# Two interleaved transformer layers on one core: a planner that keeps ACT and DVE apart in a PSUM bank, last weights placed behind the last strips, and one boot V pass moved to steps 5 to 7

## The chip, the cores and the metric

The kernel runs on one core of one Trainium2 chip. The metric is the device time of one launch in microseconds (us). A core has five engines that run their own instruction queues in order and wait for each other through semaphores: PE (TensorE, with weight loads listed apart as PEld), DVE (VectorE), ACT (ScalarE), POOL (GpSimd) and SP (SyncE). In this kernel SP and POOL issue the DMA transfers. PE writes only to PSUM, which is cut into eight banks here; ACT and DVE read the banks.

## The reference

Two layers of the same kind are applied one after the other to x, 2048 rows of 512 bfloat16 numbers. Each layer is a recurrent attention with memory (A) and a gated feed-forward block (B), both behind a layernorm:

```
for s in range(n_seg):                       # 64 segments of 32 rows, in order
    h = concat([mem, x[s]])                  # 8 memory rows + 32 rows = 40 rows
    q, k, v = h@Wq, h@Wk, h@Wv               # 32 heads of 128
    p = softmax(mask(q k^T * scale))
    o = (p @ v) @ Wo
    mem = o[:8]; out[s] = o[8:]
x = x + A(layernorm(x)); x = x + B(layernorm(x))   # B: (sigmoid(h Wg) * (h Wu)) Wd, F = 1792
x = x + A(layernorm(x)); x = x + B(layernorm(x))
```

The memory makes the 64 segments a chain: segment s+1 cannot start before the first eight rows of segment s are out.

## The kernel before, in words

**Steps.** A step t computes segment t of the first layer and, 6 steps later in time, segment t-6 of the second layer in the same matmuls (`emit_step`). So there are 70 steps. Steps 0 to 5 and 64 to 69 carry one layer (40 columns in each matmul), steps 6 to 63 carry both (80 columns). In a step, the 32 heads go in six groups (five of 6 heads, one of 2). For each group: q and k (L721), a copy of their bank by ACT, scores (L735), mask and softmax on DVE and ACT (L748 to L780), transposition of p (L794) and a copy, p times v (L807) and a copy, and the product with Wo (L824), which all groups gather in one bank, WB. At the end of a step DVE copies the memory rows from WB to the next step's hT (L837 for two layers, L842 for one), and ACT copies the other rows from the same bank to oxT (recorded as L1017, since every plain copy is issued there on ACT and at L1019 on DVE).

**v.** The rows of v that depend on the memory are made in the step itself by the "strips" (`add_strips`, L693, 32 matmuls): two banks, two copies to sst, and four DMAs on SP (L702) that lay the rows into the v tiles vsb. The rows that depend on x alone are made ahead by V passes (`v_pass`, L583): 128 rows of v at a time in eight chunks of 512 columns, four matmuls each, then a copy and a DMA to a scratch tensor scr in HBM, from which SP loads them to vsb when their step comes (L681). Nine V passes of the first layer (twelve of its sixteen blocks, in three groups of four, `v_group`) are "boot" passes: they use the nine weight tiles of the feed-forward block as staging (pool bootp, two chunks to a tile) and their DMAs go on SP or POOL. The first loads of feed-forward weights wait for these tiles. The other V passes use the small tiles vst (three of them, one chunk each) and SP.

**Feed-forward.** After every fourth step of a layer a block of 128 rows goes through `ffn`: transposes (L891), layernorm (`layernorm_T`: DVE L539 to L543, a power on POOL at L542, PE transposes L552), gate and up (L923), activation, down (L947). Weights come by DMA from POOL (L915, L916, L941) in a ring of three tiles of each kind. For the first layer, a layernorm and a V pass for the second layer follow. The last block of the second layer is done in two parts (the first three quarters while step 69 runs, the last quarter after it), with its weights all loaded once (`last_weights`, L871): nine into the ring tiles and twelve into the tile wv_sb of Wv, which is free once step 69's strips have read it.

**What sets the order.** All of this is written as tasks with engine, duration and dependencies, and a list scheduler (`Planner`) lays out the order of every engine's instructions: `forward` gives a free engine the ready task with the longest tail, with PSUM banks and buffers handed out as they come free; `backward` refines the tails; 24 rounds, and the order with the shortest plan is taken. A task's keys r and w are only the planner's view of it. The semaphore waits in the program come from the tiles that an instruction really touches and from the order. Where two engines read one bank, the program makes the second wait for the first, which this planner does not know; it only counts an extra 240 ns (`late=240.0`, L849) for the ACT copy of WB. Feed-forward and V-pass tasks without a near deadline are what fills PE while a step waits for its softmax.

Of the kernel before, what the change touches and what calls it, by code (L numbers as in the profile page):

```python
# [10 lines left out]
F32 = mybir.dt.float32  # L11
# [5 lines left out]
P = 128  # L17
MEM = 8
SEG = 32
# [7 lines left out]
BLK = 4  # L27
# [22 lines left out]


class Task:
    __slots__ = ("eng", "dur", "lat", "fn", "deps", "succ", "tail", "boost", "ndep", "ready", "start", "idx", "on", "fresh", "acq", "rel", "durs", "tick", "prev", "land", "adj")

    def __init__(self, eng, dur, lat, fn, boost):
        self.durs = dur if isinstance(dur, dict) else {e: dur for e in eng}
        self.eng, self.dur, self.lat, self.fn, self.boost = eng, min(self.durs.values()), lat, fn, boost
        self.deps, self.succ, self.fresh = set(), [], set()
        self.acq, self.rel = [], []
        self.on = None  # L60
        self.land = 3000.0
        self.adj = {}


class Buf:

    __slots__ = ("pool", "kind", "users", "first", "left", "slot", "t_free", "t_prev")

    def __init__(self, pool, kind):
        self.pool, self.kind = pool, kind  # L70
# [4 lines left out]


class Pool:
    def __init__(self, tiles, caps=None):
        self.tiles, self.caps = tiles, caps or {}
        self.free = [(0.0, None, i) for i in range(len(tiles))]  # L80
        self.used = {}


class Planner:
# [18 lines left out]
    def add(self, eng, dur, fn, r=(), w=(), lat=None, boost=0.0, use=(), late=0.0):  # L103
        engs = eng if isinstance(eng, tuple) else (eng,)
        tk = Task(engs, dur, self.LAT[engs[0]] if lat is None else lat, fn, boost)
        tk.idx = len(self.tasks)
        for k in r:
            if k in self.writer:
                tk.deps.add(self.writer[k])
                tk.fresh.add(self.writer[k])  # L110
        for k in w:
            if k in self.writer:
                tk.deps.add(self.writer[k])
            for q in self.readers.get(k, ()):
                tk.deps.add(q)
        for k in w:
            self.writer[k] = tk.idx
            self.readers[k] = []
        for k in r:
            self.readers.setdefault(k, []).append(tk.idx)  # L120
        tk.deps.discard(tk.idx)
        if late:
            tk.adj = {d: late for d in tk.fresh if self.tasks[d].eng == ("PE",)}
        self.tasks.append(tk)
        for k in list(r) + list(w) + list(use):
            if isinstance(k, Buf) and (not k.users or k.users[-1] != tk.idx):
                k.users.append(tk.idx)
        return tk
# [78 lines left out]
    def forward(self):  # L207
        T = self.tasks
        for bf in self.bufs:
            bf.first, bf.left, bf.slot, bf.t_free = None, len(set(bf.users)), None, 0.0  # L210
            bf.pool.free = [(0.0, None, i) for i in range(len(bf.pool.tiles))]
            bf.pool.used = {}
            bf.pool.last = {}
# [36 lines left out]
        while left:  # L250
            while events and events[0][0] <= now:
                _, kind, i = heapq.heappop(events)
                if kind == 0:
                    for e in T[i].eng:
                        heapq.heappush(ready[e], (-T[i].tail, i))
            did = False
            for e in free:
                if free[e] > now:
                    continue
                h, aside, tk = ready[e], [], None  # L260
                while h:
                    q = heapq.heappop(h)
                    if T[q[1]].on is not None:
                        continue
                    if T[q[1]].acq and not fits(T[q[1]], now):
                        aside.append(q)
                        continue
                    tk = T[q[1]]
                    break
                for q in aside:  # L270
                    heapq.heappush(h, q)
                if tk is None:
                    continue
                did = True
                tk.on, tk.start, tk.dur = e, now, tk.durs[e]
                seq[e] += 1
                tk.tick = seq[e]
                for bf in tk.acq:
                    pool = bf.pool
                    q = min((q for q in pool.free if self.slot_at(q, tk) <= now), key=lambda q: q[0])  # L280
                    pool.free.remove(q)
                    bf.slot = q[2]
                    tk.prev += pool.last.get(q[2], [])
                    pool.last[q[2]] = sorted(set(bf.users))
                    pool.used[bf.kind] = pool.used.get(bf.kind, 0) + 1
                end = now + tk.dur
                if self.waits(tk, seen[e]) > 1 and e in ("DVE", "ACT"):
                    end += self.WAIT
                free[e] = end
                if e == "SP":  # L290
                    lanes.append(end + tk.land)
                    if len(lanes) >= 8:
                        free[e] = max(end, lanes[-8])
                heapq.heappush(events, (free[e], 1, 0))
                for bf in tk.rel:
                    bf.left -= 1
                    if end >= bf.t_free:
                        bf.t_free, bf.first = end, tk
                    if bf.left == 0:
                        bf.pool.free.append((bf.t_free, bf.first, bf.slot))  # L300
                        bf.pool.used[bf.kind] -= 1
                        heapq.heappush(events, (bf.t_free + bf.first.lat + self.TO_PE, 1, 0))
                        heapq.heappush(events, (bf.t_free + bf.first.lat, 1, 0))
                order.append(tk)
                left -= 1
                for s in tk.succ:
                    n = T[s]
                    n.ready = max(n.ready, end + self.gap(tk, n))
                    n.ndep -= 1
                    if n.ndep == 0:  # L310
                        release(n)
            if not did and left:
                while events and events[0][0] <= now:
                    _, kind, i = heapq.heappop(events)
                    if kind == 0:
                        for e in T[i].eng:
                            heapq.heappush(ready[e], (-T[i].tail, i))
                        did = True
                if did:
                    continue  # L320
                assert events, "no task can go on"
                now = events[0][0]
# [24 lines left out]
class Kern:  # L347
# [49 lines left out]
    def setup_tiles(self):  # L397
# [43 lines left out]
        self.wd = [c.tile([P, 2, D], BF16, name=f"wd{i}") for i in range(self.ND)]  # L441
        self.lns = [c.tile([P, 12], F32, name=f"lns{i}") for i in range(3)]
        pp = ctx.enter_context(tc.tile_pool(name="ps", bufs=1, space=PSUM))
        self.bank = Pool([pp.tile([P, 512], F32, name=f"bank{i}") for i in range(8)], {"bg": 3, "v": 3})
        self.qkp = Pool(self.qku)
        self.vstp = Pool(self.vst)
        self.sstp = Pool(self.sst)
# [154 lines left out]
    def v_group(self, blocks, psts, boot=False):  # L602
# [5 lines left out]
        for b, cut in zip(blocks, cuts):  # L608
            pst, B = psts[b] if b in psts else self.ln_x(b)
            for q, c0, r0, n in cut:  # L610
                xi = (base + q) % 2
                pcs[q].append((c0, 0, b, r0, n))
                self.take_v(pst, B, 0, self.xvf[xi], [("xvf", xi, g) for g in range(c0 // 32, (c0 + 4 * n) // 32)], c0, r0, n)
            for q in range(3):
                if sum(4 * x[4] for x in pcs[q]) == P:
                    xi = (base + q) % 2
                    self.v_pass(self.xvf[xi], [("xvf", xi, g) for g in range(4)], pcs[q], boot)
                    pcs[q] = []

    def load_x(self, b, xb, key, boost=None):  # L620
# [28 lines left out]
    def emit_step(self, t):  # L649
# [194 lines left out]
        for idx, j in enumerate(jobs):  # L844
# [1 line left out]
            b = s // BLK  # L846
            oi = b % 2
            dst = self.oxT[j][oi][:, :, (s % BLK) * SEG:(s % BLK + 1) * SEG]
            pl.add("ACT", 160, lambda dst=dst, a=48 * j - c0: (dst, wo3(a, SEG)), r=[WB], w=[("oxT", j, oi, s % BLK)], late=240.0)  # L849

    def last_weights(self):

        if self.lw is None:
# [3 lines left out]
            for jp in range(self.FC // 2):  # L857
                row = []
                for nm, ring, n in (("wg", self.wg, self.NG), ("wu", self.wu, self.NG), ("wd", self.wd, self.ND)):
# [8 lines left out]
                        keys = keys + [own]  # L868
                        k += 1
                    src = self.wdv[:, 2 * jp:2 * jp + 2, :] if nm == "wd" else (self.wgv if nm == "wg" else self.wuv)[:, :, jp * 2 * P:(jp + 1) * 2 * P]  # L870
                    pl.add("POOL", 760, lambda tl=tl, src=src: nc.gpsimd.dma_start(out=tl[:, :, :], in_=src), w=keys, lat=6000.0)  # L871
                    row.append((tl, own))
                self.lw.append(row)
        return self.lw
# [94 lines left out]

    def trace(self):  # L970
        self.fill = {}
        self.lw = None
        self.clear()
        p0 = self.pre1(0)
# [12 lines left out]
        for t in range(self.NSTEPS):  # L987
            if t % BLK == 0 and t and t // BLK + 1 < self.NBLK:
                self.pre1(t // BLK + 1)
            self.emit_step(t)  # L990
            if t % BLK == BLK - 1 and t < self.NSEG:
                b = t // BLK
                if b % 3 == 0 and b <= 9:
# [83 lines left out]
```

## Time and profile before

| | |
|---|---|
| Median of 4 runs | 1859.58 us (1858.24 to 1860.54) |
| The profiled execution | 1860.49 us, its span 1858.7 us, mean granted PE clock 0.997 |
| PE busy | 1817.9 us, 98% |
| PEld, DVE, ACT, POOL busy | 1576.1, 1274.7, 1174.0, 570.6 us |
| Step start to step start, two layers, steps 18 to 21 | 23.2, 23.3, 26.6, 31.1 us |
| Step start to step start, one layer, steps 1 to 3 and 66 to 68 | 20.8, 20.1, 22.5 and 19.6, 18.9, 18.5 us |
| Step 69's strips to the end of the span | 39.6 us |

A step's start is the start of its first strips matmul (L693). "Busy" adds the records of an engine; PE's matmuls overlap in their pipeline, so a busy PE can still run below its best rate. How much it runs below is seen from the start-to-start time of matmuls of one kind: 72 q and k matmuls of 80 columns take 2.58 us in the chain of the profile, which is 35.8 ns each.

### The profile page before, as it was taken

To read this page: it belongs to the slowest core of one execution; us is meant where nothing else is said; L and a number is where in the kernel's file an instruction comes from. 1 tells how busy PE (TensorE), PEld (TensorE's weight loads), DVE (VectorE), ACT (ScalarE), POOL (GpSimd) and SP (SyncE) were. 2 spreads that over 40 slices of the span, in tenths; PEclk is the share of its full clock that TensorE was granted. 3 is DMA by queue.
4 is the path that set the end of the run, shared out by engine and by line. 5 is a ranking of instruction groups with operands and counts; after the bars stand their busy time and mean duration, and the time that the engine had idled before them with its cause. 6 is when DMAs were issued, how large, how long until landed. Compare 5 with 4: busy or idle time off the path is not lost.

```text
span 1858.7 us, 94041 instructions
## 1 busy us (share of the span) xinstructions
PE 1817.9 (98%) x41066; PEld 1576.1 (85%) x41282; DVE 1274.7 (69%) x4115; ACT 1174.0 (63%) x2748; POOL 570.6 (31%) x821
## 2 busy tenths in 40 slices
PE   8999999999999999999999999999999999999998
PEld 3678788888888898989888898989888888989786
DVE  5456566776677667767677777767677667767564
ACT  6665666666666666666666656666666666665553
POOL 4214023222424142323424142323424132324223
PEclk9999999999999999999999999999999999999998
DMA  9625234454645454554645364554645454545434
GB/s 350 231 77 166 77 98 135 138 155 129 177 129 167 120 166 125 151 150 131 182 129 166 104 182 120 150 153 127 184 127 163 120 163 120 155 141 159 143 101 132
DMA packets 128438, 273.79 MB, mean 147 GB/s; under 512 B 26882, under 2 KB 59402, under 8 KB 128026
## 3 DMA queue, kind: packets, MB, share of 16 engines
q0 software_dynamic: 56848, 183.48, 33.5%
q1 hardware_dynamic: 71178, 84.29, 15.9%
q8 instruction: 323, 5.29, 1.2%
q14 instruction: 89, 0.73, 0.1%
HBM read 221.85 MB, written 27.26 MB: 134 GB/s over the span
## 4 chain that ended last, share of the span: by engine, by line
PE 90%; SPq 3%; DVE 2%; DMA 2%; ACT 2%; issue 1%; POOL 0%; ACTq 0%; POOLq 0%; DVEq 0%
PE bank L721 32%; PE bank L824 16%; PE bank L923 11%; PE bank L693 7%; PE bank L583 7%; PE bank L735 5%; PE bank L794 4%; PE bank L947 4%; PE bank L807 4%; SPq L491 2%; PE bank L552 1%; DMA wk_sb<-in_A_Wk_dram 1%; DMA vsb<-sst 0%; DMA wv_sb<-in_A_Wv_dram 0%; PE bank L891 0%
## 5 line engine op out<-in xcount | busy, mean ns | idle before, releaser
L721 PE MATMUL bank<-hT,wq_sb 128*128 128x80 bf16 (+1 forms) x8960 | 622.1, 198 | 2.3 <-ACT hT L1017 0.7
L721 PE MATMUL bank<-hT,wk_sb 128*128 128x80 bf16 (+1 forms) x8960 | 621.1, 198 | 1.3 <-issue 1.1
L1017 ACT CAST qku<-bank 128x480 bf16<-128x480 f32 (+3 forms) x770 | 394.5, 512 | 251.7 <-PE bank L721 224.5
L721 PEld LDWEIGHTS <-wq_sb 128*128 128x128 bf16 x8960 | 458.6, 99 | 27.1 <-DVE hT L837 3.5
L721 PEld LDWEIGHTS <-wk_sb 128*128 128x128 bf16 x8960 | 450.6, 99 | 1.7 <-issue 1.2
L748 DVE TENSOR_TENSOR st<-bank,maskb 80x240 f32<-80x240 f32 (+1 forms) x732 | 269.7, 369 | 224.4 <-PE bank L735 212.5
L824 PE MATMUL bank<-otsb,wo_sb 128*128 128x80 bf16 (+1 forms) x8960 | 367.4, 198 | 6.8 <-ACT otsb L1017 3.8
L824 PEld LDWEIGHTS <-wo_sb 128*128 128x128 bf16 x8960 | 338.5, 99 | 23.7 <-issue 6.9
L915 POOL DMA_DIRECT2D wg<-in_B_w_gate_dram x217 | 165.0, 760 | 492.2 <-PE bank L923 439.2
L1017 ACT CAST otsb<-bank 128x480 bf16<-128x480 f32 (+3 forms) x420 | 200.6, 487 | 91.1 <-PE bank L807 72.1
L777 DVE TENSOR_TENSOR pb<-st,rz 80x480 bf16<-80x480 f32 x348 | 206.3, 593 | 5.5 <-PE bank L794 0.3
L760 DVE TENSOR_REDUCE sm<-st 80x6 f32<-80x240 f32 (+3 forms) x420 | 153.3, 365 | 75.3 <-ACT st L758 73.2
L542 POOL TENSOR_TENSOR lns<-lns,negh 128x1 f32<-128x1 f32 (+1 forms) x79 | 44.2, 561 | 519.6 <-DVE lns L541 432.5
L941 POOL DMA_DIRECT2D wd<-in_B_w_down_dram x217 | 153.7, 710 | 158.0 <-PE bank L735 66.2
L1017 ACT CAST ptsb<-bank 128x480 bf16<-128x480 f32 (+3 forms) x321 | 158.7, 496 | 56.7 <-PE bank L794 53.2
L758 ACT ACTIVATE st<-st 80x240 f32<-80x240 f32 (+3 forms) x420 | 160.1, 381 | 32.3 <-DVE st L755 31.4
L923 PE MATMUL bank<-xnT,wg 128*128 128x128 bf16 (+2 forms) x1784 | 172.6, 219 | 2.4 <-ACT xnT L1017 1.6
L923 PE MATMUL bank<-xnT,wu 128*128 128x128 bf16 (+2 forms) x1784 | 172.2, 219 | 0.0
L735 PE MATMUL bank<-qku 128*80 128x80 bf16 (+1 forms) x2240 | 163.3, 202 | 1.4 <-ACT qku L1017 0.3
L916 POOL DMA_DIRECT2D wu<-in_B_w_up_dram x217 | 162.4, 748 | 6.4 <-PE bank L923 2.2
L735 PEld LDWEIGHTS <-qku 128*80 128x80 bf16 (+1 forms) x2240 | 123.8, 117 | 42.2 <-ACT sst L1017 22.1
L755 DVE TENSOR_TENSOR st<-st,mx 80x240 f32<-80x240 f32 (+3 forms) x420 | 155.8, 371 | 5.0
(99 smaller groups left out, 2462.4 us busy)
## 6 DMA issues: line engine op xcount, KB each, us to landing
wg<-in_B_w_gate_dram POOLq DMA_DIRECT2D x220, 256.0 KB, 4.2
wu<-in_B_w_up_dram POOLq DMA_DIRECT2D x220, 256.0 KB, 4.7
wd<-in_B_w_down_dram POOLq DMA_DIRECT2D x220, 256.0 KB, 5.1
vsb<-scr SPq DMA_DIRECT2D x508, 48.0 KB
vsb<-sst SPq DMA_DIRECT2D x280, 64.0 KB
scr<-vst SPq DMA_DIRECT2D x128, 96.0 KB
wq_sb<-in_A_Wq_dram SPq DMA_DIRECT2D x5, 768.0 KB
wk_sb<-in_A_Wk_dram SPq DMA_DIRECT2D x5, 768.0 KB
```

The costliest lines, as they stand in the source:

```text
L721: nc.tensor.matmul(o_ap, lhsT=W[:, c, h * P:(h + 1) * P], rhs=mv(c), start=(c == 0), stop=(c == DC - 1))
L735: nc.tensor.matmul(s_all(SB)[pr, uh - h0 + i, :], lhsT=qku[:, i, 0, 0:ncol], rhs=qku[:, i, 1, 0:ncol], start=True, stop=True)
L748: pl.add("DVE", dve_ns(n, True), lambda gsz=gsz, hs=hs, st=st, SB=SB, pj_=pj_, npj_=npj_, mk=mk, idx=idx: nc.vector.tensor_tensor(out=st[p ...
L755: pl.add("DVE", dve_ns(n), lambda gsz=gsz, hs=hs, st=st, mx=mx: nc.vector.tensor_tensor(out=st[pr, hs], in0=st[pr, hs], in1=mx[pr, hs].uns ...
L758: pl.add("ACT", act_ns(n), lambda hs=hs, st=st: nc.scalar.activation(out=st[pr, hs], in_=st[pr, hs], func=ACTF.Exp, scale=self.scale), r=s ...
L777: nc.vector.tensor_tensor(out=o, in0=st[pr, hs].unsqueeze(1).to_broadcast([npart, 2, gsz, L]), in1=rz[pr, :, 0:gsz].unsqueeze(3).to_broadc ...
L824: nc.tensor.matmul(WB[:, c * ncol:(c + 1) * ncol], lhsT=self.wo[:, h, c * P:(c + 1) * P], rhs=otsb[:, hl, 0:ncol], start=(h == 0 and c == ...
L915: pl.add("POOL", 760, lambda wg=wg, fs=fs: nc.gpsimd.dma_start(out=wg[:], in_=self.wgv[:, :, fs]), r=[("wo", self.H - 1)], w=[gk] + bt, la ...
L916: pl.add("POOL", 760, lambda wu=wu, fs=fs: nc.gpsimd.dma_start(out=wu[:], in_=self.wuv[:, :, fs]), r=[("wo", self.H - 1)], w=[uk] + bt, la ...
L923: nc.tensor.matmul(gu[:, 2 * i + k, 0:n], lhsT=W[:, c, i * P:(i + 1) * P], rhs=xnT[:, c, rw], start=(c == 0), stop=(c == DC - 1))
L941: pl.add("POOL", 760, lambda wd=wd, ip=ip: nc.gpsimd.dma_start(out=wd[:], in_=self.wdv[:, 2 * ip:2 * ip + 2, :]), w=[dk] + (["boot"] if se ...
L1017: nc.scalar.copy(out=dst, in_=src)
```

## The change

Three edits. (1) The planner learns that ACT and DVE must not read one bank at the same time: a task that reads a bank is put aside while the other engine is reading it, and the earlier reader counts among the waits; the fixed 240 ns goes. (2) In `last_weights`, the twelve loads into the tile of Wv are given the v tiles of step 69's strips as keys they read, so that the planner places them after the strips' DMAs. (3) One of the nine boot V passes (third group, pass 2, for blocks 13 and 14) is kept back and added after step 4, as an ordinary V pass that also reads the memory rows of step 5's hT as a key.

```diff
         self.tasks.append(tk)
+        if engs[0] != "PE":
+            tk.banks = tuple(k for k in r if isinstance(k, Buf) and k.pool.psum)
...
                     if T[q[1]].acq and not fits(T[q[1]], now):
                         aside.append(q)
                         continue
+                    held = [bf.rd[1] for bf in T[q[1]].banks if bf.rd and bf.rd[0] != e and bf.rd[1] > now]
+                    if held:
+                        aside.append(q)
+                        heapq.heappush(events, (max(held), 1, 0))
+                        continue
...
+                for bf in tk.banks:
+                    if bf.rd and bf.rd[0] != e:
+                        tk.prev.append(bf.rd[2])
                 end = now + tk.dur
...
+                for bf in tk.banks:
+                    bf.rd = (e, end + self.LAT[e], tk.idx)
...
-                    self.v_pass(self.xvf[xi], [("xvf", xi, g) for g in range(4)], pcs[q], boot)
+                    args = (self.xvf[xi], [("xvf", xi, g) for g in range(4)], pcs[q])
+                    if self.late == (blocks[0], q):
+                        self.held = args
+                    else:
+                        self.v_pass(*args, boot)
...
-            pl.add("ACT", 160, lambda dst=dst, a=48 * j - c0: (dst, wo3(a, SEG)), r=[WB], w=[("oxT", j, oi, s % BLK)], late=240.0)
+            pl.add("ACT", 160, lambda dst=dst, a=48 * j - c0: (dst, wo3(a, SEG)), r=[WB], w=[("oxT", j, oi, s % BLK)])
...
-                    pl.add("POOL", 760, lambda tl=tl, src=src: nc.gpsimd.dma_start(out=tl[:, :, :], in_=src), w=keys, lat=6000.0)
+                    pl.add("POOL", 760, lambda tl=tl, src=src: nc.gpsimd.dma_start(out=tl[:, :, :], in_=src), w=keys, lat=6000.0,
+                           r=[("vs", (4 * (self.NSTEPS - 1) + q) % 5) for q in range(4)] if k else [])
...
+        self.late = (10, 2)
...
             self.emit_step(t)
+            if t == 4:
+                tile, keys, pieces = self.held
+                self.v_pass(tile, keys + [("hT", (t + 1) % self.R, 0, "m")], pieces)
```

No task is added or taken away. The number of PE instructions is the same, 41,282 weight loads and 41,282 matmuls; the kept-back pass is staged in eight tiles of one chunk instead of four of two, so it issues 16 DMAs of half the size, all on SP.

## The prediction

> **What bounds the kernel now.** I read the page's busy row and its slices first.
>
> ```profile
> PE 1817.9 (98%) x41066; PEld 1576.1 (85%) x41282; DVE 1274.7 (69%) x4115; ACT 1174.0 (63%) x2748; POOL 570.6 (31%) x821
> ...
> PE   8999999999999999999999999999999999999998
> ...
> PEclk9999999999999999999999999999999999999998
> ...
> q8 instruction: 323, 5.29, 1.2%
> ```
>
> PE is never idle in any slice, but "busy" hides how fast it runs. So next the chain of waits in the middle (start us, us, what), for pitches:
>
> ```profile
> 1371.01 2.58 PE bank L721 x72
> 1373.59 0.23 PE bank L735 x6
> ...
> 1376.63 1.84 PE bank L693 x32
> ```
>
> 72 matmuls of 80 columns in 2.58 us are 35.8 ns each; strips cost 1.84 us; in the timeline, matmuls of 40 columns start every 25 ns, of 128 every 56, of 512 every 216. With these pitches I added the work of every step in the built order and set it against the trace's time from strips to strips. All work is 1770 us of the span's 1858.7; 89 us are not covered. Of these, 16 lie before step 1's strips (first data, weight loads), 21 in steps 1 to 7, 25 in the 56 steps 8 to 63 (mostly 0.25 each, the change from strips to scores), 14 in steps 64 to 68, 13 after step 69's strips. PE's work is not altered; the change can only move these 89 us.
>
> Two places matter. Step 7 and step 8, by stretches (bounds, length, busy time of PE, PEld, DVE, ACT, POOL with counts, clock, DMA share, GB/s):
>
> ```profile
> 228.10:248.50 20.40, 18.67 (x463) 16.62 (x461) 12.89 (x44) 12.60 (x28) 0.00 (x0) 1.00 0.15 37
> 248.50:273.50 25.00, 24.80 (x590) 22.89 (x590) 18.30 (x63) 15.75 (x36) 8.66 (x12) 1.00 0.47 130
> ...
> 1826.10:1829.50 3.40, 1.97 (x66) 1.76 (x63) 2.85 (x10) 1.76 (x6) 2.86 (x4) 1.00 1.04 305
> 1829.50:1839.80 10.30, 9.05 (x177) 8.01 (x174) 4.45 (x16) 4.47 (x14) 0.72 (x1) 0.50 0.48 141
> ```
>
> Step 7 has no filler at all: 17.1 us of work in 20.4, 3.3 uncovered; step 8, filled, leaves 0.7. The other rows are step 69: PE works 1.97 of 3.40 us, and then its clock is at half for 10.2 us, the only such stretch in the span. PE's timeline shows the holes (last bracket: idle time before, and releaser):
>
> ```profile
> 1828.82 0.26 PE L794 MATMUL bank<-ident,pb 40*128 40x40 bf16 x4 [1.43 <-issue]
> ...
> 1836.05 0.96 PE L824 MATMUL bank<-otsb,wo_sb 128*128 128x40 bf16 x24 [1.25 <-ACT th L928]
> ```
>
> "Issue" means that no semaphore is waited for. Queue q8 (packets, MB, share) brought 323 packets of 16 KB; PE has 82,564 loads and matmuls, 323 times 256. The packets are PE's instructions. Setting each packet against the moment when PE reaches the block that it brings, 320 of 323 end at least 1.0 us ahead. The three others (0.2 us late to 0.5 ahead) are exactly the hole at 1828.8, the one at 1836.05, and one of 1.12 us at 154.3. They began 2.8, 6.4 and 2.8 us after the previous block was entered; mid-span packets began 0.7 after, on average. All three fell into bursts of weight loads (over 210 GB/s on POOL's queue), and into code of 40 columns, where PE eats 256 instructions in about 4 us.
>
> **The V pass.** It is eight chunks of four matmuls, 6.9 us. In the two built orders, the fillers of step 0 shrink by one chunk, step 2 from eight to five, step 3 from five to one; step 5 gains two, step 7 six. Step 7 then has 5.2 us more work for its 3.3 us of holes, and I give it the remainder of step 8: 3.3 - 0.6 = 2.7 us gained. In step 5 one chunk (0.86 us) now stands between the last transposes of block 0 and step 6's first q, where the timeline has
>
> ```profile
> 188.58 0.40 PE L552 MATMUL bank<-ident,xn 128*128 128x128 bf16 x4 [0.45 <-DVE xn L543]
> 189.73 0.30 PE L721 MATMUL bank<-hT,wq_sb 128*128 128x80 bf16 x4 [0.75 <-ACT hT L1017]
> ```
>
> so it covers the second wait: 0.9 gained with the start-up. Lost: step 3 with 1.1 us of filler resembles step 66 (2.2 us of filler, 3.5 uncovered), and has 3.3 already: 0.4, at most 1.2. Step 2 becomes like step 1 (the same five chunks, 2.1 against 2.0): nothing. The order of step 10 has p times v followed directly by its own L824 at two more places; each lacks about half of the 0.85 us of copy and signalling between them: 1.0 lost. The eight bank copies (0.59 us each) move with the chunks; DVE and ACT are 63% and 62% busy in step 7, so the next matmul pays nothing unless a copy delays q's copy on ACT, bound 1 us. The pass's 16 DMAs go past SP, where loads of v rows for step 8 (L681) and strips' rows (L702) queue behind them. An issue takes about 0.6 us and waits for its chunk's copy; the loads have some 10 us until step 8 multiplies by v. I take 0; if that cover is gone, the nearest wait is 1.3 us at 212. The boot tiles come free four chunks earlier in the order, so the first feed-forward loads do too; their burst met the late packet at 154.3. It may miss the next block or hit it: 0, bounds -1.2 and +1.2. Sum of this part: -2.7 - 0.9 + 0.4 + 1.0 = -2.2.
>
> **The last weights.** The new key adds no wait on the chip: in both programs the twelve loads wait for their DMA lane and PE alone, not for SP's DMAs. What holds them is POOL's order. They stand behind the power of the last block's layernorm:
>
> ```profile
> 1820.32 0.56 POOL L542 TENSOR_TENSOR lns<-lns,negh 96x1 f32<-96x1 f32 x1 [1.57 <-DVE lns L541]
> 1820.84 0.79 POOL L871 DMA_DIRECT2D wv_sb<-in_B_w_gate_dram  x1
> ...
> 1821.69 2.42 SPq L702 DMA_DIRECT2D vsb<-sst  x4
> ```
>
> Before, the transposes that start this layernorm stand ahead of step 69's strips (1819.1), and the loads begin 1.7 us after the strips' start, ahead of the rows. Now they stand behind strips and two q groups, 1.8 + 1.25 us in; the power comes 2.7 us later as before, and the first load starts at 5.8. The rows, issued at 2.6 to 5.0, go first, and the short block whose packet was late is entered at 5.8 with the nine ring loads landed (the last at 1823.7, 4.6 after the strips) and one load just starting. So its packet is in time: 1.43 gained, and the clock does not drop. The next block is entered in full burst; packets under over 200 GB/s began 1.7 us after entry on average, which is in time, so its 1.25 goes too. The half clock cost 8 ns on each of some 137 small matmuls (24 of L824 take 0.96 us against 0.76 in the first steps) and 30 on each of 40 of L923: 2.3. Together 5.0; if the second packet is as late as before, only 1.5. I take 4.0. Price: what queues behind the delayed loads on POOL is only the last quarter's power, 20 us later; the first matmul on these weights stood at 1840.3, 15.5 us after the first landing, so 4.1 later is covered, and if not, PE waits for the difference. The last quarter's layernorm has fewer down matmuls behind which to hide: 0.5 lost. Sum: -3.5.
>
> [...]
>
> **One reader per bank.** No instruction changes. The chip already keeps the readers apart (ACT's oxT waited 53.6 us in all for DVE's L837 copy, with PE busy). Only orders differ. Counting pairs that stand too close for the 0.85 us of their copy, steps 8 to 63 have 3.8 us of shortfall in either order: 0, bounds -1.5 and +1.5. In step 66 the shortfalls drop by 1.0, but only 2.5 us of PE work now stand between group 3's scores and its transposition (L794), and the softmax chain between them has 2.6 us of durations plus its hops, on a DVE shared with three other groups: an estimated gap of 1 to 2 us in one piece, say 1.5, +0.5 net. [...]
>
> **Sum.** -2.2 - 3.5 + 0.5 = -5.2 against the profiled 1860.49, of which 1.8 lie around the span: 1855.3. The runs' median is 0.9 below that execution, so 1859.58 - 5.2 = 1854.4 us.
>
> **Rivals.** *The last step keeps its holes* (the packets are late at other places in the same burst, the clock drops again): the second part gives +0.5 instead of -3.5, time 1858.4. For it: twelve loads still run under instruction-hungry code. Against: the tightest block is out of the burst. Chance 0.28. *The moved pass gains nothing*: fillers are used in step 7 and missing in steps 10 to 14, where steps of 1.7 us uncovered exist already (14, 26, 38); the first part becomes 0, time 1856.6. Chance 0.10. *Slower*: the gap in step 66 halves the clock and code of 40 columns does not bring it back. Each such step has 480 matmuls, 8 ns more each, 3.8 us a step, with its feed-forward work at half rate about 6. From one and a half steps on it outweighs the gain by more than 0.2%; through step 69, 1868. For it: three windows of 3.4 us passed before the clock rose again. Against: it did rise, in poorer code. Chance 0.06. The forecast has 0.56.
>
> **How the numbers follow.** 0.2% is 3.7 us, about what a measurement of this kernel tells from no change: faster means under 1855.9. The forecast's range is 1850.5 (5.0 at the end, 1.2 at 154, 1.5 in the middle) to 1856.5, so most of it is faster; with a share of the second rival 0.58. Same 0.36, slower 0.06. The overall range takes in the first rival with a unit above it: 1850.5 to 1859.5.
>
> **What would show it.** PE's granted clock at 1.00 throughout step 69; no idle "issue" over 1 us at an L794 there; first L871 load into wv_sb about 5.8 us after the last strips' start; step 7 some 22.6 us long with six L583 chunks and step 8's length unchanged; the sum of steps 8 to 63 unchanged within 1.5 us. I am wrong if half clock appears in step 66 or 69, or if steps 10 to 14 grow by what step 7 saved.

## The result and the profile after

The changed kernel takes 1856.88 us (median of 35 runs, 1854.59 to 1860.73), the kernel before 1859.35 us beside it (55 runs, 1855.24 to 1863.99). The ratio is 0.9987, interval 0.9982 to 0.9992: 2.5 us saved (1.5 to 3.3), about half of the 5.2 that were forecast. The profiled execution took 1856.03 us with a span of 1854.3; against the profiled execution of before that is 4.5 us. It lies 0.9 under its median and the one of before 1.1 over its own, so a comparison of the two profiles flatters the change by 2 us.

The page after, with the rows that answer to those shown of before:

```profile
PE 1817.0 (98%) x41069; PEld 1575.7 (85%) x41282; DVE 1270.4 (69%) x4163; ACT 1166.1 (63%) x2700; POOL 569.4 (31%) x817
...
PE   8999999999999999999999999999999999999999
...
PEclk9999999999999999999999999999999999999999
...
q8 instruction: 323, 5.29, 1.3%
```

Work and packets are the same; only the last slice differs. By stretches (bounds, length, busy time with counts of PE, PEld, DVE, ACT, POOL, clock, DMA share, GB/s), first steps 7 and 8 of the changed kernel:

```profile
221.10:243.80 22.70, 22.54 (x489) 18.76 (x493) 16.41 (x53) 15.84 (x35) 0.55 (x1) 1.00 0.27 72
243.80:269.10 25.30, 24.79 (x591) 22.71 (x596) 17.58 (x56) 15.60 (x36) 8.86 (x12) 1.00 0.55 153
```

Step 7 is 22.7 us long, as forecast (22.6), and PE works in 22.54 of them instead of 18.67 of 20.40. Step 8 is 0.3 us longer than before. Then the burst of last loads in step 69, where before PE worked 1.97 of 3.40 us and then ran at half clock for 10.2:

```profile
1825.50:1836.00 10.50, 10.50 (x295) 9.57 (x292) 8.68 (x33) 6.64 (x22) 7.00 (x10) 1.00 0.94 292
```

292 GB/s, and PE has no hole and its full clock. On POOL the first load into wv_sb starts 6.2 us after the last strips (1817.5), behind the same power:

```profile
1823.06 0.65 POOL L555 TENSOR_TENSOR lns<-lns,negh 96x1 f32<-96x1 f32 x1 [4.01 <-DVE lns L554]
1823.67 0.79 POOL L888 DMA_DIRECT2D wv_sb<-in_B_w_gate_dram  x1
```

But step 66 has a new stretch at half clock. First the whole step before the change and after it, whose mean clock is 0.82, then the two parts of it that matter:

```profile
1762.10:1781.70 19.60, 18.87 (x554) 16.71 (x550) 12.50 (x43) 11.49 (x33) 2.08 (x3) 1.00 0.24 66
1761.20:1780.30 19.10, 17.58 (x489) 15.50 (x490) 11.27 (x40) 10.28 (x30) 2.08 (x3) 0.82 0.22 59
...
1764.30:1767.71 3.41, 2.48 (x62) 2.02 (x58) 2.89 (x11) 1.55 (x6) 0.00 (x0) 1.00 0.32 79
1767.71:1774.53 6.82, 6.23 (x156) 5.90 (x157) 3.42 (x15) 3.45 (x12) 0.55 (x1) 0.50 0.12 34
```

In the third row PE stands idle from 1766.8 to the row's end and on to 1768.05, between group 5's scores and group 3's L811 (the former L794). The timeline of PE:

```profile
1766.55 0.22 PE L752 MATMUL bank<-qku 128*40 128x40 bf16 x2
1768.05 0.38 PE L811 MATMUL bank<-ident,pb 40*128 40x40 bf16 x6 [1.27 <-DVE pb L797]
```

Where the uncovered time went, step by step as in the prediction (a step's time less its matmuls at the prediction's pitches, us):

| steps | before | after | change | forecast |
|---|---|---|---|---|
| ahead of step 0 | 12.3 | 11.8 | -0.5 | 0 |
| 0 to 7 | 24.4 | 20.2 | -4.2 | -3.2 |
| 8 to 63 | 24.8 | 27.4 | +2.6 | +1.0 |
| 64 to 67 | 11.5 | 13.9 | +2.4 | +0.5 |
| 68 and 69 | 15.5 | 10.9 | -4.6 | -3.5 |

Both ends gained more than forecast; the middle and step 66 took it back.

### The profile page after: what moved, and what is told of

It reads as the page before. It is cut to its first block, busy times and chain, and to the rows that moved or that the text cites. A ratio compares the mean times of both kernels' runs of the same rounds, so it can differ in the third digit from the quotient of the medians.

```text
span 1854.3 us, 94296 instructions
## 1 busy us (share of the span) xinstructions
PE 1817.0 (98%) x41069; PEld 1575.7 (85%) x41282; DVE 1270.4 (69%) x4163; ACT 1166.1 (63%) x2700; POOL 569.4 (31%) x817
## 4 chain that ended last, share of the span: by engine, by line
PE 92%; DVE 5%; issue 1%; ACT 1%; DMA 0%; POOL 0%; SPq 0%; ACTq 0%; DVEq 0%; POOLq 0%
PE bank L738 32%; PE bank L841 16%; PE bank L941 11%; PE bank L596 9%; PE bank L710 7%; PE bank L752 5%; PE bank L811 4%; PE bank L965 4%; PE bank L824 4%; PE bank L565 1%; DVE st L765 1%; DVE pb L794 1%; DVE mx L770 0%; DVE sm L777 0%; DVE st L772 0%
## 5 line engine op out<-in xcount | busy, mean ns | idle before, releaser
L794 DVE TENSOR_TENSOR pb<-st,rz 80x480 bf16<-80x480 f32 x348 | 205.4, 591 | 3.4
L1039 ACT CAST ptsb<-bank 128x480 bf16<-128x480 f32 (+3 forms) x298 | 151.4, 512 | 49.7 <-PE bank L811 46.0
```

The source lines that it names most:

```text
L794: nc.vector.tensor_tensor(out=o, in0=st[pr, hs].unsqueeze(1).to_broadcast([npart, 2, gsz, L]), in1=rz[pr, :, 0:gsz].unsqueeze(3).to_broadc ...
L1039: nc.scalar.copy(out=dst, in_=src)
```

## Experiments

Theory: the three edits act separately; late instruction packets under the burst made the holes of step 69, and PE being too little at work there halved the clock; in the changed kernel the same happens in step 66, because the bank rule thinned it. Rivals: the gain at the end comes from the other order of PE's work, not from the burst; the half clock has another cause, or costs nothing; the V pass gives back what it saves. Each time stands beside that of the kernel before, measured together with it. The mean granted clock of all runs of a kernel is given as well: 0.001 less means 3.7 us at half clock. It was 0.9975 for the kernel before and 0.9980 after.

**The edits one by one.** The V pass alone (kernel before, plus the two hunks on `self.held`):

```
+                    if self.late == (blocks[0], q):
+                        self.held = args
...
+            if t == 4:
+                tile, keys, pieces = self.held
+                self.v_pass(tile, keys + [("hT", (t + 1) % self.R, 0, "m")], pieces)
```

> Only the V pass is put off; the other two edits are not made. In the built order steps 8 to 69 are nearly those of the kernel before, so the end is untouched. If the parts are separate, as the prediction had it: step 7 some 22.6 us long, 2.0 to 3.0 us saved in all (1856.4 to 1857.4), the holes of 1.43 and 1.25 us and the 10 us of half clock in step 69 still there. If the saving of step 7 is given back in steps 8 to 14 as fillers run short: no change (within 0.7 us of the kernel before).

Measured: 1857.68 beside 1859.09, ratio 0.9994 (0.9987 to 1.0), clock 0.9981. So 1.1 us by the ratio and 1.4 by the medians, and the interval reaches none. Step 7 was 22.1 us, and step 69 kept its holes and its half clock. In the profile, steps 0 to 7 had 18.3 us uncovered, and steps 8 to 63 had 28.6 against 24.8. Step 10 lost 1.3 and step 12 0.4; the rest came in small pieces and in instruction packets that were late in mid-span, for which PE shows

```profile
1108.72 0.32 PE L725 MATMUL bank<-hT,wk_sb 128*128 128x80 bf16 x4 [0.39 <-issue]
```

The three other kernels with the moved V pass and without the bank rule (they follow below) have such a hole at this place too: 0.74, 1.28 and 1.01 us of idle time.

The new key alone:

```
-                    pl.add("POOL", 760, lambda tl=tl, src=src: nc.gpsimd.dma_start(out=tl[:, :, :], in_=src), w=keys, lat=6000.0)
+                    pl.add("POOL", 760, lambda tl=tl, src=src: nc.gpsimd.dma_start(out=tl[:, :, :], in_=src), w=keys, lat=6000.0,
+                           r=[("vs", (4 * (self.NSTEPS - 1) + q) % 5) for q in range(4)] if k else [])
```

> Only the new key of the twelve last loads. Steps 0 to 67 keep their order, step 66 has its 2.2 us of filler. If late instruction packets under the burst made the holes and the half clock of step 69, and the later start of the burst removes them: 3.5 to 4.5 us saved (1855 to 1856), clock 1.00 throughout steps 66 to 69. If the holes belong to the code of step 69 and not to the burst: they stay, within 0.7 us of the kernel before.

Measured: 1856.98 beside 1859.09, ratio 0.9987 (0.998 to 0.9993), clock 0.9990. 2.1 to 2.4 us, under what was expected, though the profile shows what was meant: 11.4 us uncovered in steps 68 and 69, no hole without a releaser, and the full clock under the burst:

```profile
1828.40:1839.00 10.60, 10.60 (x290) 9.28 (x286) 8.35 (x32) 6.84 (x22) 7.81 (x11) 1.00 0.96 299
```

The key alone has the ratio of the whole change, 0.9987.

The bank rule alone:

```
+                    held = [bf.rd[1] for bf in T[q[1]].banks if bf.rd and bf.rd[0] != e and bf.rd[1] > now]
...
-            pl.add("ACT", 160, lambda ..., w=[("oxT", j, oi, s % BLK)], late=240.0)
+            pl.add("ACT", 160, lambda ..., w=[("oxT", j, oi, s % BLK)])
```

> Only the rule of one bank reader at a time. It changes orders in steps 2 to 65 and leaves steps 66 to 69 as they were. The prediction's part for it: 0, at most 1.5 us either way, half clock only in step 69 as before. If the rule costs the 2 us by which steps 15 to 63 of the changed kernel were longer: 1.5 to 2.5 us slower.

Measured: 1859.41 beside 1859.09, ratio 1.0001 (0.9992 to 1.001). Nothing, and steps 8 to 63 have 24.7 us uncovered against 24.8: steps 14, 26 and 38 win 0.65 each, many others lose 0.1 to 0.3.

**Pairs of edits.** Without the bank rule:

> The changed kernel without the bank rule: the V pass put off and the new key of the last loads only. Step 66 then has the order of before (2.2 us of filler, 3.2 us of matmul work between group 3's scores and its L794) instead of the thin order (1.3 and 2.5 us). If the bank rule thinned step 66 and with it brought the half clock there: no half clock in step 66 or 69 and the sum of the two parts measured alone, -1.1 and -2.1 us against the kernel before: 1855.5 to 1856.2, 1 us under the changed kernel. If the bank rule costs nothing: the time of the changed kernel, 1856.9.

Measured: 1855.24 beside 1859.53 (7 runs), ratio 0.9974 (0.9962 to 0.9985), clock 0.9989. That is 4.3 us saved, 1.8 more than by the whole change. The two intervals overlap a little, so that the rule costs time inside the change is likely, and not shown by this pair alone. And one expectation fails: the profiled execution was at half clock for 6.83 us in step 66 here too. The order of before can do that as well, only not always: two of these 7 runs have a clock of 1.0, and none of the 35 of the changed kernel is over 0.999. Without the key:

> The changed kernel without the new key: V pass put off and bank rule only. Step 66 has the order of before, step 69 too. If the parts add: 1859.1 - 1.2 + 0.3, that is 1858 to 1858.5, with the issue holes and the half clock of step 69, and clear of half clock in step 66 in most phases. The key is then worth 1.1 to 1.6 us inside the change, against 2.1 to 2.4 alone, because with the bank rule it thins step 66. If the key kept its full worth in the change: 1859 or more.

Measured: 1858.42 beside 1859.18, ratio 0.9997 (0.9989 to 1.0006), clock 0.9969; the holes of step 69 are back (1.38 and 1.56 us of idle time). As expected: the key is worth some 1.5 us inside the change. It takes the key and the bank rule together to thin step 66: with either alone its filler (feed-forward work) stays at 2.2 us, with both it is 1.3.

**The burst.** The kernel before with less in the burst: each of the twelve last loads brings only 16 of its 128 partitions, so the last block is computed with weights that are partly not its own:

```
+                    rows = 16 if own[0] == "lw" else P
-... nc.gpsimd.dma_start(out=tl[:, :, :], in_=src) ...
+... nc.gpsimd.dma_start(out=tl[0:rows, :, :], in_=src[0:rows]) ...
```

> The kernel before with the twelve last loads into wv_sb cut to 16 of 128 partitions, an eighth of their bytes; the other rows keep the old contents, so the last block's output is computed on other weights. Order and count of all instructions stay. If the burst makes the packets late and they make the holes and the half clock: no issue hole over 0.5 us in step 69, clock 1.00, 3.5 to 5 us saved (1854.5 to 1856). If packets are late whatever the load, or the half clock comes from the code itself: the time within 0.7 us of the kernel before, half clock again after 1829.

Measured: 1855.06 beside 1859.09, ratio 0.9978 (0.9971 to 0.9986), clock 0.9988. No instruction moved, and 4.1 us are gone. The stretch of the former holes:

```profile
1830.00:1844.00 14.00, 14.00 (x392) 12.66 (x390) 10.19 (x34) 8.62 (x29) 2.35 (x5) 1.00 0.09 23
```

Then the burst whole, but later, with the order of the other four engines kept:

```
+        def touch(q):
+            v = self.vsb[(4 * (self.NSTEPS - 1) + q) % 5]
+            return self.nc.gpsimd.tensor_copy(out=self.scrat[0:P, q:q + 1], in_=v[0:P, 0:1])
...
+        return order[:first] + rest + ts + moved + order[last + 1:]
```

> The kernel before, order of PE, ACT, DVE and SP untouched; only POOL reads one column of each of the four v tiles of step 69 (four copies of 128x1) before the first of the twelve last loads, so these wait in fact for the strips' rows, and start some 7 us after the strips instead of 1.7. If the burst's place alone makes packets late: the hole of 1.4 to 2.0 us at the third or fourth L794 of step 69 goes, and with it most of the half clock; 2 to 4 us saved, 1855 to 1857, like the new key alone (-2.1). If the gain of the new key came from the other order of PE's work in step 69: no change within 0.7 us.

Measured: 1854.88 beside 1859.53, ratio 0.9974 (0.9965 to 0.9983), clock 0.9996: 4.6 us, twice the key alone. POOL now really waits for the strips' rows, and the first load starts 7.7 us after the strips (1818.8):

```profile
1823.45 0.70 POOL L1027 COPY scrat<-vsb 128x1 bf16<-128x1 bf16 x2 [2.89 <-DMA vsb<-sst]
1825.81 0.53 POOL L1027 COPY scrat<-vsb 128x1 bf16<-128x1 bf16 x2 [1.65 <-DMA vsb<-sst]
1826.48 0.79 POOL L875 DMA_DIRECT2D wv_sb<-in_B_w_gate_dram  x1
```

PE then works through the burst without a hole and at full clock:

```profile
1826.00:1836.00 10.00, 10.00 (x298) 9.27 (x295) 7.72 (x28) 6.93 (x24) 9.16 (x14) 1.00 0.74 219
```

So it is the burst's place, not PE's order, that makes the packets late here. The order that comes with the key is no help at the end: steps 68 and 69 have 9.8 us uncovered here and 11.4 with the key alone, where the loads start 8.4 us after the strips. With the key, the last quarter's layernorm has fewer down matmuls to hide it and leaves PE waiting. Two of these waits in the kernel with the key alone are

```profile
1846.17 0.26 PE L552 MATMUL bank<-ident,xn 32*128 32x32 bf16 x4 [0.16 <-DVE xn L543]
1846.78 0.25 PE L924 MATMUL bank<-xnT,wg 128*128 128x32 bf16 x4 [0.35 <-ACT xnT L1018]
```

**The clock.** All half-clock stretches of an execution start and end on one grid with a step of 3.41 us: in the profile of before 10.24 us from 1829.53, three steps, and the next from 1860.25, behind the span's end, nine steps after the first; in that of after 6.83 us from 1767.71, two steps, and the next from 1853.04, 25 steps after. The grid's phase differs from execution to execution (by 0.4 us between these two, each counted from its span's start). For each window of the grid the columns streamed by the recorded matmuls were counted (the columns of its output, 80 for one that writes 128x80). Matmuls of 512 columns start every 216 ns here, those of 80 every 36: 180 ns for 432 columns, 2.4 columns per ns (the expectations write 2.4 GHz for it). At that rate a window of 3.41 us has room for 8,192 columns, and the count is given as a share of that. (Windows with strips come out above 1, since 32 of those matmuls, 512 columns each, take 1.84 us.) In the kernel before, the window from 1826.1 has 0.305, the next three, at half clock, have 0.38, 0.30 and 0.43, and then the clock is back. To see whether columns or idle time decide, blocks of 280 matmuls that nobody reads were put without a gap into three steps of the kernel before:

```
+            self.nc.tensor.matmul(self.bank.tiles[slot][:, 0:w], lhsT=self.ident[:], rhs=self.wq[:, 0, 0:w], start=True, stop=True)
...
+                    self.spot[tk.idx] = {20: 4, 30: 20, 40: 28}[t]
```

> The clock by itself. In the kernel before, 280 matmuls that nobody reads are put behind the scores of group 5 in three steps: of 4 columns in step 20, 20 columns in step 30, 28 columns in step 40. At about 25 ns each they keep PE issuing without an idle gap for 7 us, two windows, at 0.07, 0.33 and 0.47 of the columns that 2.4 GHz allows. If the clock follows the columns streamed in a window of 3.41 us (bound near 0.40): half clock in steps 20 and 30, none in 40. If only idle time of PE brings it down, be it 1.4 us or 3.4 us: no half clock in any of the three. The time is some 21 us longer, and more at half clock.

Measured: 1886.72 us, a single execution. The blocks of 4 and of 20 columns halved the clock. That of 28 did not, though two late packets brought its lowest window down to 0.38. Windows of the first block and what followed, then of the second, then of the third (PE's busy time is the second number after the bounds):

```profile
575.38:578.79 3.41, 3.41 (x141) 3.41 (x139) 1.35 (x5) 0.00 (x0) 0.00 (x0) 1.00 0.33 118
578.79:585.60 6.81, 6.75 (x141) 6.57 (x139) 0.00 (x0) 1.58 (x3) 0.00 (x0) 0.50 0.09 24
851.80:855.30 3.50, 3.50 (x143) 3.48 (x140) 0.55 (x1) 0.00 (x0) 0.00 (x0) 0.99 0.00 0
855.30:858.70 3.40, 3.40 (x78) 3.40 (x75) 0.00 (x0) 0.26 (x1) 0.00 (x0) 0.50 0.11 34
...
1118.00:1122.00 4.00, 3.54 (x142) 3.45 (x139) 0.00 (x1) 0.00 (x0) 0.00 (x0) 1.00 0.07 20
```

In the first block PE was busy for all of 3.41 us, and still the clock fell: no idle gap is needed. In the third it stood idle for 0.46 of 4.00 us, and the clock stayed. Now step 66 of the changed kernel, filled with five matmuls of 512 columns behind group 5's scores (the same helper, `rhs=self.wq[:, 0, 0:512]`):

> The changed kernel with five matmuls of 512 columns, whose result nobody reads, put into step 66 behind the scores of group 5, where PE waits 1.3 us for the probabilities of group 3. They take 5 x 0.216 = 1.1 us of that wait. In the six profiles so far, the clock halves for one window of 3.41 us exactly when the window before it, on a fixed grid, had streamed under 0.40 of the columns that 2.4 GHz allows (0.20 to 0.395 eleven times; 0.416 and more, never). The five add 0.31 of a window to step 66's 0.31. If that rule holds: no half clock in step 66, mean clock up from 0.998 to 0.999, 1 to 2 us saved against the changed kernel: 1855 to 1856. If the half clock comes from something else in step 66, or costs nothing: 1856.9.

Measured: 1854.17 beside 1859.53 (6 runs), ratio 0.9972 (0.996 to 0.9983), clock 0.9998. That is 2.7 us under the changed kernel (the intervals of the two ratios just touch). Steps 66 and 67 took 38.1 us instead of 40.2; the window on the former gap:

```profile
1765.85:1769.26 3.41, 2.87 (x56) 1.89 (x55) 3.41 (x15) 1.71 (x6) 0.00 (x0) 1.00 0.18 41
```

PE still has 0.5 us of holes in it, and the clock stays. Its twin with 43 matmuls of 4 columns:

> The twin of the filled step 66: at the same place 43 matmuls of 4 columns instead of five of 512. They keep PE issuing for the same 1.1 us, but stream 172 columns instead of 2560 (0.02 of a window instead of 0.31). If the columns streamed in the window decide: step 66 halves the clock as in the changed kernel, mean clock near 0.998, and the time stays at that of the changed kernel, 2 us or more over the filled one. If an idle gap decides, or if the five helped only by shifting later work: half clock gone or time as in the filled one, some 5 us under the kernel before.

Measured: 1856.79 beside 1859.07, ratio 0.999 (0.9982 to 0.9998), clock 0.9978, the time of the changed kernel. No run of it has a clock over 0.998, and none of the filled kernel one under 0.999. PE in the same place, the window that ends at 1769.61, and what follows:

```profile
1767.40 1.23 PE L1039 MATMUL bank<-wq_sb,ident 128*128 128x4 bf16 x43
```

```profile
1766.20:1769.61 3.41, 3.14 (x87) 2.66 (x84) 3.01 (x12) 1.52 (x6) 0.00 (x0) 1.00 0.33 76
1769.61:1776.40 6.79, 6.65 (x166) 6.45 (x166) 2.28 (x12) 3.50 (x12) 0.55 (x1) 0.50 0.11 34
```

Of the two windows, this one is the busier (3.14 us against 2.87), and it has fewer columns (0.25 against 0.48): it is the one that is followed by half clock. The fourteen profiles of this case have 7,511 windows clear of start and end: all 23 under 0.38 were followed by half clock, none of the 7,469 over 0.415, and 11 of the 19 in between. The same bound holds for the way back: every half-clock window with over 0.415 was followed by full clock.

**Towards a faster version.** The V pass with the real wait, and the same with two matmuls of 512 columns (the same helper) where step 66 waits 0.44 us for an output copy:

> The V pass put off, and instead of the new key and the bank rule the real wait for the strips' rows (four small reads on POOL). Measured alone the two gave -1.1 to -1.4 and -4.6 us. If they add up: 1853.0 to 1854.0 at 1859.3 for the kernel before, the fastest version but for step 66's half clock, which the order of before meets in one phase of the grid in five. If the V pass gives back in steps 8 to 63 what it saves before (3 us more uncovered there in the profile of the V pass alone, against 6 saved in steps 0 to 7): no better than the real wait alone, 1854.9.

> The same with two matmuls of 512 columns that nobody reads in step 66, where PE waits 0.44 us for group 0's output copy. They add 0.125 to windows that hold 0.38 to 0.46. If the column count rules: no half clock in step 66 in any execution, mean clock at or above 0.999, and 0.2 to 0.7 us under the version without them (the half clock falls on step 66 there only in a part of the executions). If not, the same time.

Measured: 1854.22 and 1854.26 beside 1859.07, ratios 0.9974 (0.9965 to 0.9982) and 0.9972 (0.9963 to 0.9981), clock 0.9993 and 1.0. On top of the real wait (0.9974) the V pass brings nothing that can be told. With the two matmuls all 11 runs have a clock of 1.0, against 6 of 11 without them, but the median is no better. The filled step 66, the real wait and these two stand within 0.7 us of each other, 4.6 to 5.4 under the kernel before and 2 to 2.7 under the change.

## Why the prediction was half right

- *The last weights, -3.5.* The mechanism holds: packets late under the burst (a smaller burst takes the holes away and saves 4.1 us, a later one too, 4.6), the first short block out of it, the half clock gone. Measured alone it is 2.1 to 2.4, interval 1.3 to 3.7, so the term was probably oversized, by about 1. The two profiles say 4.6; the medians decide.
- *Step 66, +0.5, and the clock left out of the sum.* This is the step that failed. The gap of 1 to 2 us came as estimated (1.27), and 6.83 us of half clock with it, for which the sum holds nothing (the rival "Slower" has it, at 0.06). The gap's length says little of that: in the kernel before, one of 1.12 us at 154 left the clock alone. The window at 154 holds 0.45 of its columns, that of step 66 0.32, and the bound lies near 0.40. The filled step measures the price of the half clock as 2.1 us in steps 66 and 67, since the filling only takes the place of the wait. With 2.1 more, the sum would have been -3.1. In these runs half clock came and went on the grid of 3.41 us, behind windows with under about 0.40 of their columns, with a gap of 1.27 us (step 66, 0.32) or with none (the block of 4-column matmuls, 0.07).
- *The V pass, -2.2.* Steps 0 to 7 did as forecast: step 7 -3.1 (2.7), step 5 -1.4 (step 6's start -0.9 in the prediction), step 3 -0.25 (+0.4), the hole at 154 gone (0, at best -1.2). That last gain is luck of the execution: the kernel without the key, which moves the pass too, has such a hole of 0.66 at 148. Step 10 lost 1.05 (1.0). The queue of SP was put at 0, and a cost of it is not shown: the wait for strips' rows, 1.14 us idle at 212 before, is 1.81 at 205 after, but 0.78 with the V pass alone. What the sum had not was the rest of steps 8 to 63: some 1.5 us more, in orders that change far from the moved pass and in packets late in mid-span. Alone the pass gave 1.1 to 1.4.
- *The bank rule, 0±1.5 in steps 8 to 63.* Right: -0.1 in its own profile, +0.2 in time (-1.5 to 1.9). That it thins step 66 only together with the key was in the built order, not in the reasoning.
- *The rivals.* The last step does not keep its holes. "The moved pass gains nothing" named 1856.6, close to the 1856.88 measured, but that is luck: the pass alone gave 1.1 to 1.4 us (an interval that reaches none), and what was missing came from step 66 and the last weights too. The slow case did not come: the clock returns after two windows (6.83 us).

Open: why some packets are late in mid-span, where the 4 us ahead of such a hole moved anything from 115 to 300 GB/s. In the holes without a releaser, the packet had mostly begun 2.2 to 2.9 us before PE went on, and landed 1.1 to 1.7 before; nothing tried here moves them at will. Also open is the rest of the 2.3 us by which the real wait beats the key: the waits of the last layernorm are about 0.9 of it in the key's profile (0.5 in that of the changed kernel, as forecast), and the intervals overlap a little.

## What to carry to other kernels

Where code streams few columns per matmul, put the clock into the cost of a gap too: count the columns around it. Here a wait that brought a window of 3.41 us under about 0.40 of 8,192 columns cost itself and then 6.83 us (step 66 after) or 10.24 us (step 69 before) at half clock. Wide matmuls that nobody reads, put into the wait, kept the clock and cost nothing that can be told. And set a forecast against the medians: a single execution of the kernel before lay up to 4.6 us off its median, and the two profiled ones alone flattered the change by 2 us.

## What was not expected of the hardware

- In these runs the clock followed columns, not PE's busy time: 3.41 us of gapless 4-column matmuls (0.07) halved it, and 28-column ones with 0.46 us of idle time in 4.00 did not.
- The grid's phase was another one from execution to execution (by 0.4 us between the profiles of before and after). In the order of before, the lowest window of step 66 comes to 0.38 to 0.46; five of ten profiled executions with that order were at half clock there. Six of the fourteen profiles also have a half-clock window between 150 and 218 us, where the kernel before happened to have none. A part of the runs' spread goes with this: in 61 runs of the kernel before, clock and time have a correlation of -0.64, and runs at 0.996 or less are 2.7 us or more over those at 0.998.
- A burst of 12 loads, 256 KB each, cost 4 to 5 us at its place (4.1 saved with an eighth of the bytes, 4.6 when it came later). Started 6 us later it left PE without a hole and at full clock.
